# First two chunks' tokens in one load, transposed together ahead of all products

## Chip, cores, metric

One core of a Trainium2 chip runs the whole program. The metric is the device time of one execution in microseconds. Time before: 343.93 us, median of three runs (343.65 to 343.94); the profile of it that is read below is of an execution of 343.26 us. "us from the start" below counts from the start of the profile's span.

## The reference

Two independent attention blocks, A and B, of the same shape, their outputs side by side:

```python
# B=16, Sq=32, D=1024; Hq=32, Hkv=4, Sk=512, Dh=128; all bfloat16
q = (x @ wq).reshape(B, Sq, Hq, Dh).transpose(0, 2, 1, 3)
k, v = (jnp.repeat(c, Hq // Hkv, axis=1) for c in (k_cache, v_cache))
p = softmax(einsum("bhqd,bhkd->bhqk", q, k) * Dh ** -0.5)
o = einsum("bhqk,bhkd->bhqd", p, v).transpose(0, 2, 1, 3).reshape(B, Sq, Hq * Dh)
out = o @ wo          # for A and for B, then concatenate([a, b], axis=-1)
```

## The kernel before

A's tokens x are 512 rows of 1024 values. The product with wq needs x transposed, in eight chunks of 128 columns. The first four chunks come by plain loads (two chunks to a load) and are transposed on PE, the rest by transposing DMAs. While the first loads are on their way, PE runs dummy products on a constant (`warm_up`), because PE starts at a lower clock (the traces below show products 107 ns apart at first and 54 ns later), which activity is to lift. P is 128, TT is 4 (blocks of 128 tokens), DC is 8 chunks, HC is 4, REP is 8 and NF is 6 (heads).

The early loads, all issued by SP in this order:

```python
def load_x(d0, t0, t1):
    nc.sync.dma_start(
        out=x_sb[:, t0:t1, d0 * P:(d0 + 2) * P],
        in_=x_v[:, t0:t1, d0 * P:(d0 + 2) * P],
    )

# ... load_x_transposed and load_w0 cut: a load through the transposing DMA, and a load of weights ...

nc.scalar.preload_act_table_set("natural_log_exp_and_others")
load_x(0, 0, TT // 2)
load_w0(0, 1, 0, NF // 2)
load_x(0, TT // 2, TT)
load_w0(0, 1, NF // 2, NF)
load_w0(1, 2, 0, NF)
load_x(2, 0, TT)
load_w0(2, 3, 0, NF)
load_w0(3, 4, 0, NF)
# ... later loads cut ...
```

PE's order at the start. `first_heads(heads, chunks, t0, t1)` makes the products of these heads and chunks for token blocks t0 to t1, so a full one has 512 columns:

```python
def warm_up(n):
    for _ in range(n):
        nc.tensor.matmul(
            first_q[HALF][:, 0:P], lhsT=warm, rhs=warm, start=True, stop=True
        )

def transpose_x(d, t0, t1, copy, ps=None):
    if ps is None:
        ps = psum.tile([P, NTOK], BF16, name="xT_ps", tag="ob")
    for tt in range(t0, t1):
        nc.tensor.transpose(
            ps[:, tt * P:(tt + 1) * P], x_sb[:, tt, d * P:(d + 1) * P], ident[:]
        )
    ts = slice(t0 * P, t1 * P)
    copy(out=xT[0][:, d, ts], in_=ps[:, ts])

def first_heads(heads, dcs, t0=0, t1=TT):
    ts = slice(t0 * P, t1 * P)
    for dc in dcs:
        for h in heads:
            nc.tensor.matmul(
                first_q[h][:, ts],
                lhsT=w0[dc // HC][:, dc % HC, h * DH:(h + 1) * DH],
                rhs=xT[0][:, dc, ts],
                start=(dc == 0 and t0 == 0),
                stop=(dc == DC - 1),
            )

warm_up(22)
for tt in range(2):
    transpose_x(0, tt, tt + 1, nc.vector.tensor_copy)
transpose_x(1, 0, 2, nc.scalar.copy, spare)
warm_up(2)
first_heads((0, 1, 2), (0,), 0, 1)
transpose_x(0, 2, TT, nc.vector.tensor_copy)
transpose_x(1, 2, TT, nc.scalar.copy)
first_heads((0, 1, 2), (0,), 1, 2)
warm_up(1)
first_heads((0, 1, 2), (0,), 2, TT)
first_heads((3, 4, 5), (0,), 0, 2)
first_heads((3, 4, 5), (0,), 2, TT)
first_heads(range(0, NF - 2), (1,))
transpose_x(2, 0, TT, nc.vector.tensor_copy)
transpose_x(3, 0, TT, nc.scalar.copy)
# ... chunks 2 to 7, then the stream of all other products ...
```

B's tokens come much later, planned into slots of the main loop (about 2.33 us each):

```python
def load_xT_b(d0, d1):
    if d0 == 0:
        xT[1] = blk_tile([P, DC, NTOK], "xT")
    nc.sync.dma_start_transpose(
        out=xT[1][:, d0:d1, :],
        in_=B_x.flatten_outer_dims()[:, d0 * P:d1 * P],
    )

for n in range(2):
    at(GRP * (n + 3) - 2, load_xT_b, n * HC, (n + 1) * HC)
```

## Time and profile before

| what | value | view |
|---|---|---|
| span | 341.5 us | page, first line |
| PE busy | 337.4 us, 99% | page, part 1 |
| chain of waits | PE 99% | page, part 4 |
| PE starts | 0.93 us | timeline |
| first half of the tokens landed | 3.01 us | the trace's issues and landings |
| weights of chunk 1 landed | 6.10 us | the same |
| unbroken stream of products starts | 7.47 us | timeline |
| last product starts | 338.1 us | timeline |

The page of the kernel before: span, busy time of each engine, and the chain of work that ended last.

```profile
span 341.5 us, 5512 instructions
...
PE 337.4 (99%) x2130; PEld 214.4 (63%) x2130; DVE 265.6 (78%) x337; ACT 185.8 (54%) x209; POOL 46.7 (14%) x206
...
PE 99%; ACT 0%; issue 0%; ACTq 0%
```

PE is busy 99% of the time, and everything that ended last is PE's. In the trace, from 7.47 us to the last product, each 512-column product starts 216 ns after the one before it, with no gap. So nothing after 7.47 us can be won by better loads. Only the start can change.

The start on PE, from the timeline (start in us, duration of the group in us, instruction, out<-in, form, count):

```profile
0.93 2.52 PE L516 MATMUL q_ps<-const-bfloat16-1.0 128*128 128x128 bf16 x22 [0.93 <-PEq L700]
3.24 0.63 PE L524 MATMUL xT_ps<-ident,x_sb 128*128 128x128 bf16 x4
3.67 0.42 PE L516 MATMUL q_ps<-const-bfloat16-1.0 128*128 128x128 bf16 x2
3.88 0.53 PE L534 MATMUL q_ps<-xT,w_sb 128*128 128x128 bf16 x3
4.20 0.63 PE L524 MATMUL xT_ps<-ident,x_sb 128*128 128x128 bf16 x4
4.63 0.46 PE L534 MATMUL q_ps<-xT,w_sb 128*128 128x128 bf16 x3
4.93 0.22 PE L516 MATMUL q_ps<-const-bfloat16-1.0 128*128 128x128 bf16 x1
5.00 2.19 PE L534 MATMUL q_ps<-xT,w_sb 128*128 128x256 bf16 x13
7.02 0.61 PE L524 MATMUL xT_ps<-ident,x_sb 128*128 128x128 bf16 x8
7.47 1.70 PE L534 MATMUL q_ps<-xT,w_sb 128*128 128x512 bf16 x7
```

Read it with three things in mind.

- L516 are dummies, L524 transposes, L534 the products of q. Useful work starts at 3.24 us, and three more dummies lie in the middle.
- The durations of matmuls overlap (the four transposes from 3.24 us take up to 0.31 us each but start 107 ns apart), so starts say more. 22 dummies start between 0.93 and 3.13 us (four transposes follow at 3.24), one every 107 ns; the eight transposes from 7.02 to 7.42 us start one every 56 ns. In this execution the step from 107 to 54 ns came at 4.88 us, where the trace's record of the granted clock begins. The page's clock row and the windows view show full clock from the first slice on, although starts are 107 ns apart there: only the starts tell of the slow phase.
- A group of one engine can hide a gap. The 13 products from 5.00 us contain one, from 5.98 to 6.15 us, in which PE has nothing to do.

What ended that gap stands in PE's weight loads (who waited for whom; us in total, times, longest):

```profile
PEld L534 <- DMA w_sb<-in_A_wq_dram: 0.3, 1, 0.3
PEld L524 <- DMA x_sb<-in_A_x_dram: 0.3, 1, 0.3
```

The wait for w_sb is the gap: chunk 1's weights landed at 6.10 us. The wait for x_sb is no loss: the weight load of the next transposes waited for tokens that landed at 6.92 us, but PE was still streaming the product before it and the transposes started on time at 7.02 us.

### The profile page before, as it was taken

What the parts mean: (1) busy time and instruction counts of PE and PEld (TensorE: products, weight loads), DVE (VectorE), ACT (ScalarE), POOL (GpSimd) and SP (SyncE); (2) the same over time, 40 slices, a digit from 0 to 9 for tenths busy, and PEclk for the clock granted to TensorE, in tenths of its full rate; (3) what the DMA queues carried; (4) which work ended last, traced back from release to release, by engine and by line L of the source; (5) the groups of instructions that cost most, each with busy time, mean ns of one, the idle gap of its engine ahead of it and who ended that gap; (6) DMA issues with size and microseconds to landing.
All of it is one profiled execution on the core that took longest, in us unless ns stands there. A gap on an engine that the chain in (4) does not pass through costs nothing.

```text
span 341.5 us, 5512 instructions
## 1 busy us (share of the span) xinstructions
PE 337.4 (99%) x2130; PEld 214.4 (63%) x2130; DVE 265.6 (78%) x337; ACT 185.8 (54%) x209; POOL 46.7 (14%) x206
## 2 busy tenths in 40 slices
PE   8999999999999999999999999999999999999996
PEld 7455666666666666666666666666666666666555
DVE  1046988888988898888888988879888888889540
ACT  3058666666667667666645545555555555555110
POOL 0001110011111111110012221222122101111100
PEclk9999999999999999999999999999999999999999
DMA  6999999989996987999999955998649998440001
GB/s 194 300 192 262 295 264 196 238 244 267 277 247 154 232 232 223 192 313 263 316 272 290 280 148 142 334 270 239 117 109 291 354 186 180 98 113 6 18 18 33
DMA packets 128094, 71.70 MB, mean 210 GB/s; under 512 B 75840, under 2 KB 127296, under 8 KB 128064
## 3 DMA queue, kind: packets, MB, share of 16 engines
q1 hardware_dynamic: 127536, 70.21, 84.3%
q0 software_dynamic: 384, 1.05, 0.8%
q8 instruction: 17, 0.28, 0.3%
q14 instruction: 13, 0.11, 0.1%
q10 hardware_dynamic: 144, 0.07, 0.1%
HBM read 50.86 MB, written 2.10 MB: 155 GB/s over the span
## 4 chain that ended last, share of the span: by engine, by line
PE 99%; ACT 0%; issue 0%; ACTq 0%
PE f_ps L320 32%; PE q_ps L301 28%; PE ob L425 16%; PE s_ps L357 16%; PE q_ps L534 4%; PE q_ps L516 1%; PE xT_ps L524 0%; ACT o_sb L329 0%; ACTq L329 0%
## 5 line engine op out<-in xcount | busy, mean ns | idle before, releaser
L365 ACT ACTIVATE p_sb<-s_ps,shift 128x1024 bf16<-128x1024 f32 x128 | 142.6, 1114 | 97.7 <-PE s_ps L357 85.1
L376 DVE TRANSPOSE_TENSOR_REDUCE parts<-p_sb 128x32 f32<-128x1024 bf16 x128 | 158.7, 1240 | 20.9 <-ACT p_sb L365 19.3
L320 PE MATMUL f_ps<-wo_sb,oT 128*128 128x512 bf16 (+1 forms) x544 | 132.3, 366 | 0.0
L301 PE MATMUL q_ps<-xT,wq_sb 128*128 128x512 bf16 x448 | 116.9, 379 | 0.0
L425 PE MATMUL ob<-p_sb,v_sb 128*128 128x256 bf16 x512 | 76.8, 273 | 0.0
L357 PE MATMUL s_ps<-qT,kT 128*128 128x256 bf16 x512 | 76.8, 273 | 0.0
L320 PEld LDWEIGHTS <-oT 128*128 128x128 bf16 x544 | 53.2, 98 | 35.3
L357 PEld LDWEIGHTS <-kT 128*128 128x128 bf16 x512 | 56.9, 113 | 28.3
L301 PEld LDWEIGHTS <-wq_sb 128*128 128x128 bf16 x448 | 43.8, 98 | 32.2
L425 PEld LDWEIGHTS <-v_sb 128*128 128x128 bf16 x512 | 50.1, 98 | 20.0
L447 DVE TENSOR_TENSOR oT<-r,ob 128x512 bf16<-128x512 f32 x64 | 43.9, 686 | 20.0 <-PE ob L425 19.4
L411 DVE STREAM_TRANSPOSE r<-rall 128x512 f32<-128x512 f32 x64 | 44.2, 691 | 1.1
L309 ACT CAST qT<-q_ps 128x512 bf16<-128x512 f32 x56 | 32.6, 583 | 16.6 <-PE q_ps L301 16.6
L394 POOL COPY half<-cs 64x32 f32<-64x32 f32 x32 | 6.5, 204 | 232.1 <-DVE cs L384 232.0
L329 ACT CAST o_sb<-f_ps 128x512 bf16<-128x512 f32 (+1 forms) x17 | 9.5, 558 | 23.6 <-PE f_ps L320 23.6
L534 PE MATMUL q_ps<-xT,w_sb 128*128 128x512 bf16 (+2 forms) x73 | 14.9, 359 | 0.0
L384 DVE TENSOR_REDUCE cs<-parts 128x32 f32<-128x128 f32 x32 | 12.0, 376 | 1.1
L406 DVE RECIPROCAL rall<-sums 128x32 f32<-128x32 f32 x32 | 10.2, 319 | 3.3 <-POOL sums L403 3.3
L534 PEld LDWEIGHTS <-w_sb 128*128 128x128 bf16 x73 | 7.1, 102 | 6.8 <-DMA w_sb<-in_A_wq_dram 0.3
L566 DVE CAST qT<-q_ps 128x512 bf16<-128x512 f32 x4 | 2.5, 683 | 10.2 <-PE q_ps L534 10.2
L331 POOL DMA_DIRECT2D out_dram<-o_sb x8 | 4.6, 574 | 29.3 <-ACT o_sb L329 29.3
L395 POOL TENSOR_TENSOR half<-half,cs 64x32 f32<-64x32 f32 x32 | 7.8, 243 | 2.6
(25 smaller groups left out, 46.1 us busy)
## 6 DMA issues: line engine op xcount, KB each, us to landing
v_sb<-in_A_v_cache_dram SPq DMA_DIRECT2D x16, 512.0 KB, 5.7
wq_sb<-in_B_wq_dram SPq DMA_DIRECT2D x8, 1024.0 KB, 5.7
wo_sb<-in_A_wo_dram SPq DMA_DIRECT2D x8, 1024.0 KB, 7.1
v_sb<-in_B_v_cache_dram SPq DMA_DIRECT2D x16, 512.0 KB, 4.6
wo_sb<-in_B_wo_dram SPq DMA_DIRECT2D x8, 1024.0 KB, 8.1
wq_sb<-in_A_wq_dram SPq DMA_DIRECT2D x5, 1024.0 KB, 5.9
wq_sb<-in_A_wq_dram SPq DMA_DIRECT2D x2, 512.0 KB, 7.3
kT<-in_A_k_cache_dram SPq DMA_TRANSPOSE x64, 4.4
```

Source lines behind the costliest of these rows:

```text
L301: nc.tensor.matmul(ps[:], lhsT=w[:, dc, (h % 4) * DH:(h % 4 + 1) * DH], rhs=xT[pr][:, dc, :], start=(dc == 0), stop=(dc == DC - 1),)
L309: nc.scalar.copy(out=qT[pr, g][:, :, hl, :], in_=ps[:].rearrange("p (b s) -> p b s", s=SQ),)
L320: nc.tensor.matmul(ps[:, 0:width], lhsT=oT[pr, tt][:, h, :], rhs=wo_tiles[pr, nh, h // REP][:, h % REP, off:off + width], start=(h == 0), ...
L357: nc.tensor.matmul(s_ps[:, c, :], lhsT=kT[:, i % GRP, c, :], rhs=qT[pr, g][:, b, :, :].rearrange("p h s -> p (h s)"), start=True, stop=True,)
L365: nc.scalar.activation(out=p_sb[:], in_=s_ps[:], func=ACTF.Exp, bias=shift[:], scale=SCALE)
L376: nc.vector.tensor_reduce(out=parts[k][:, q, :, :].rearrange("p c h -> p (c h)"), in_=st[i]["p"][:].rearrange("p c (h s) -> p (c h) s", s=SQ),
L384: nc.vector.tensor_reduce(out=cs[:], in_=parts.pop(k)[:].rearrange("p q c h -> p q h c"), axis=AX.X, op=ALU.add,)
L406: nc.vector.reciprocal(out=rall[:, k, :], in_=quad.pop(k)[:])
L411: nc.vector.transpose(out=r[:].rearrange("p n s -> p (n s)"), in_=rall[:, k, o * 2 * REP:(o + 1) * 2 * REP] .unsqueeze(2).to_broadcast([P, ...
L425: nc.tensor.matmul(ob[j][:, q, :], lhsT=v_sb[:, i % GRP, c, :], rhs=st[i]["p"][:, c, :], start=(c == 0), stop=(c == KC - 1),)
L447: nc.vector.tensor_tensor(out=out, in0=rcp.pop(j)[:].rearrange("p (q h) s -> p q h s", h=REP), in1=ob.pop(j)[:].rearrange("p q (h s) -> p ...
L534: nc.tensor.matmul(first_q[h][:, ts], lhsT=w0[dc // HC][:, dc % HC, h * DH:(h + 1) * DH], rhs=xT[0][:, dc, ts], start=(dc == 0 and t0 == 0 ...
```

## The change

The two first token loads of 128 KB become one of 256 KB, so each early load behind them moves up one place in SP's queue. All eight transposes of chunks 0 and 1 come ahead of all products, the dummies all go to the front (23 instead of 22 + 2 + 1). B's tokens are transposed by DMA in three pieces instead of two.

```diff
--- before.py
+++ after.py
@@ -461,11 +461,9 @@
             x_v = A_x.flatten_outer_dims().rearrange("(t p) d -> p t d", p=P)
             wq_v = A_wq.rearrange("(c p) n -> p c n", p=P)
 
-            def load_x(d0, t0, t1):
-                nc.sync.dma_start(
-                    out=x_sb[:, t0:t1, d0 * P:(d0 + 2) * P],
-                    in_=x_v[:, t0:t1, d0 * P:(d0 + 2) * P],
-                )
+            def load_x(d0):
+                ds = slice(d0 * P, (d0 + 2) * P)
+                nc.sync.dma_start(out=x_sb[:, :, ds], in_=x_v[:, :, ds])
 
             def load_x_transposed(d0):
                 nc.sync.dma_start_transpose(
@@ -480,12 +478,11 @@
                 )
 
             nc.scalar.preload_act_table_set("natural_log_exp_and_others")
-            load_x(0, 0, TT // 2)
+            load_x(0)
             load_w0(0, 1, 0, NF // 2)
-            load_x(0, TT // 2, TT)
             load_w0(0, 1, NF // 2, NF)
             load_w0(1, 2, 0, NF)
-            load_x(2, 0, TT)
+            load_x(2)
             load_w0(2, 3, 0, NF)
             load_w0(3, 4, 0, NF)
             load_w0(0, HC, NF, REP)
@@ -539,19 +536,13 @@
                             stop=(dc == DC - 1),
                         )
 
-            warm_up(22)
-            for tt in range(2):
-                transpose_x(0, tt, tt + 1, nc.vector.tensor_copy)
-            transpose_x(1, 0, 2, nc.scalar.copy, spare)
-            warm_up(2)
-            first_heads((0, 1, 2), (0,), 0, 1)
-            transpose_x(0, 2, TT, nc.vector.tensor_copy)
-            transpose_x(1, 2, TT, nc.scalar.copy)
-            first_heads((0, 1, 2), (0,), 1, 2)
-            warm_up(1)
-            first_heads((0, 1, 2), (0,), 2, TT)
-            first_heads((3, 4, 5), (0,), 0, 2)
-            first_heads((3, 4, 5), (0,), 2, TT)
+            warm_up(23)
+            transpose_x(0, 0, TT // 2, nc.vector.tensor_copy)
+            transpose_x(0, TT // 2, TT, nc.vector.tensor_copy)
+            transpose_x(1, 0, TT, nc.scalar.copy, spare)
+            for ts in ((0, TT // 2), (TT // 2, TT)):
+                first_heads(range(0, NF // 2), (0,), *ts)
+            first_heads(range(NF // 2, NF), (0,))
             first_heads(range(0, NF - 2), (1,))
             transpose_x(2, 0, TT, nc.vector.tensor_copy)
             transpose_x(3, 0, TT, nc.scalar.copy)
@@ -609,8 +600,8 @@
                     in_=B_x.flatten_outer_dims()[:, d0 * P:d1 * P],
                 )
 
-            for n in range(2):
-                at(GRP * (n + 3) - 2, load_xT_b, n * HC, (n + 1) * HC)
+            for n, (d0, d1) in enumerate(((0, 2), (2, 5), (5, DC))):
+                at(GRP * (n + 3) - 2, load_xT_b, d0, d1)
             for nh in range(NH):
                 for hg in range(HKV):
                     at(NG - 12 + nh * 8 + hg * 2, load_wo, 0, nh, hg)
```

## The prediction

> **What bounds the kernel now.** The page gives PE 99% busy of a 341.5 us span; the chain of waits is 99% PE. Start to start, the trace's matmuls run without a bubble from 7.47 us to the last at 338.1 us (a 512-column product every 216 ns). So only the time until PE reaches this unbroken stream can change. In the timeline before it, PE starts 22 dummy products at 0.93 us; 128-column instructions start every 107 ns until the granted clock rises at 4.88 us, every 54 to 56 ns after. The Trainium skill ("TensorE: Matmul & The Clock Gate", What's actually happening) says about 3.4 us of sustained activity, in a free-running window, lift the clock; here it took 3.95 us.
>
> Losses after the first tokens land (3.0 us): 3 more dummies (about 0.29 us) and 0.17 us of PE idleness (5.98 to 6.15 us) waiting for chunk 1's weights, which land at 6.10 us. The next chunks' tokens land at 6.92 us, 0.1 us before PE wants them.
>
> **What the change does.** Columns of products and number of transposes are the same. Dummies go from 25 to 23, all in front. Two 128 KB token loads (issued 0.74 and 1.75 us, landed 3.01 and 4.04 us) become one of 256 KB. An issue takes SP 0.43 to 0.50 us whatever its size, so every later early load is issued about 0.48 us sooner: chunk 1's weights at 2.2 instead of 2.73 us, the next tokens at 2.7 instead of 3.20 us. Copies of transposed tokens fall from 7 to 6, all hidden. B's tokens come in 3 pieces instead of 2 in slots where PE has no bubble; the last should land around 73 us and is needed around 83 us (estimate from slots of 2.33 us): no effect.
>
> **On the critical path.** The 256 KB land at about 3.6 us (estimate: the first half-load's 2.27 us plus 128 KB at the 215 GB/s seen from 2 to 3 us). Dummies end at 0.93 + 23 x 0.107 = 3.39 us, so PE idles about 0.2 us. Then 8 transposes and 24 column blocks (32 units of 128) lie before chunk 1: about 12 cold until 4.88 us, 20 warm, ending at about 5.98 us, the same point as now, but with chunk 1's weights landed (about 5.7 us) and the next tokens soon after (about 6.5 us). What is won is the 0.17 us bubble: gain 0.1 to 0.3 us, 0.05%, of the order of the runs' spread (343.65 to 343.94).
>
> **Prediction:** 343.75 us, 343.2 to 344.3. Faster by over 2%: 0.002; within 2%: 0.99; slower by over 2%: 0.008.
>
> **What would show it.** First token load lands at 3.4 to 3.8 us; PE idle 0.1 to 0.4 us before the first transpose; chunk 1's weights land at 5.6 to 5.9 us, no PE idleness before their products; the unbroken stream begins near 7.3 us (now 7.47); afterwards nothing but a shift.
>
> **What would make it wrong.** (1) The clock rises later: the idle gap and eight transposes in a row fall in the activity window, and the skill (same page, Part 4) says transposes do not count as PE-busy; a rise one window (3.4 us) later would cost about 1.5 us. (2) The early loads are limited by bandwidth, not issue (DMA share 0.93 to 0.99 from 4 to 7 us), so they land no sooner: gain near zero. (3) The first load lands after 4.0 us. (4) A later load with little to spare now (chunk 2's weights, 7.43 us) becomes the new wait.

## The result and the profile after

Six runs each: 343.80 us (343.12 to 344.13) against 343.53 us (343.27 to 343.94) before. The ratio is 1.0002, 95% interval 0.9989 to 1.0016: the same. (A ratio here is the mean time of one kernel's runs over the mean of the other's of the same rounds, so not quite the ratio of the medians.)

The page and the start on PE after the change (L513 dummies, L521 transposes, L531 products):

```profile
span 341.4 us, 5456 instructions
...
PE 335.2 (98%) x2083; PEld 213.7 (63%) x2122; DVE 265.5 (78%) x336; ACT 185.6 (54%) x208; POOL 46.7 (14%) x206
...
PE 97%; DMA 1%; issue 1%; ACT 0%; ACTq 0%
```

```profile
0.93 2.63 PE L513 MATMUL q_ps<-const-bfloat16-1.0 128*128 128x128 bf16 x23 [0.93 <-PEq L691]
3.74 1.04 PE L521 MATMUL xT_ps<-ident,x_sb 128*128 128x128 bf16 x8 [0.18 <-DMA x_sb<-in_A_x_dram]
4.57 2.56 PE L531 MATMUL q_ps<-xT,w_sb 128*128 128x256 bf16 x13
6.96 0.61 PE L521 MATMUL xT_ps<-ident,x_sb 128*128 128x128 bf16 x8
7.63 1.70 PE L531 MATMUL q_ps<-xT,w_sb 128*128 128x512 bf16 x7
```

Who waited for whom among PE's weight loads, up to 40 us:

```profile
PEld L521 <- DMA x_sb<-in_A_x_dram: 0.4, 1, 0.4
```

The tokens landed at 3.69 us, and PE idled from 3.35 to 3.74 us (the wait for x_sb, 0.4 us at the weight load). The wait for chunk 1's weights is gone: they landed at 5.79 us, and their first product started at 6.10 instead of 6.15 us. (In this trace the first product of the stream has no record; its weight load at 7.36 us stands where before's stands at 7.42 us. 39 matmul records are missing in all, 2083 beside 2122 weight loads; the other 8 by which the count lies below before's 2130 are two dummies and six products fewer.) The last product starts at 338.04 instead of 338.11 us. So in this pair of executions 0.06 us are won at the start, and nothing after it but that shift.

0.06 us is about a sixteenth of the spread of the changed kernel's runs, which is 1.0 us. The profile says where a gain could lie, but not why six runs of one program differ by 1 us. That became the main question.

### The profile page after: what moved, and what is told of

Read it like the earlier page. It is cut to its first block, busy times and chain, and to the rows that moved or that the text cites. A ratio compares the mean times of both kernels' runs of the same rounds, so it can differ in the third digit from the quotient of the medians.

```text
span 341.4 us, 5456 instructions
## 1 busy us (share of the span) xinstructions
PE 335.2 (98%) x2083; PEld 213.7 (63%) x2122; DVE 265.5 (78%) x336; ACT 185.6 (54%) x208; POOL 46.7 (14%) x206
## 4 chain that ended last, share of the span: by engine, by line
PE 97%; DMA 1%; issue 1%; ACT 0%; ACTq 0%
PE f_ps L320 32%; PE q_ps L301 28%; PE ob L425 17%; PE s_ps L357 16%; PE q_ps L531 4%; DMA x_sb<-in_A_x_dram 1%; PE xT_ps L521 0%; ACT o_sb L329 0%; ACTq L329 0%
## 5 line engine op out<-in xcount | busy, mean ns | idle before, releaser
L320 PE MATMUL f_ps<-wo_sb,oT 128*128 128x512 bf16 (+1 forms) x525 | 128.2, 366 | 0.6
L301 PE MATMUL q_ps<-xT,wq_sb 128*128 128x512 bf16 x430 | 113.2, 379 | 0.5
L531 PE MATMUL q_ps<-xT,w_sb 128*128 128x512 bf16 (+1 forms) x65 | 14.1, 374 | 0.1
L531 PEld LDWEIGHTS <-w_sb 128*128 128x128 bf16 x67 | 6.6, 100 | 6.9
```

The source lines that it names most:

```text
L301: nc.tensor.matmul(ps[:], lhsT=w[:, dc, (h % 4) * DH:(h % 4 + 1) * DH], rhs=xT[pr][:, dc, :], start=(dc == 0), stop=(dc == DC - 1),)
L320: nc.tensor.matmul(ps[:, 0:width], lhsT=oT[pr, tt][:, h, :], rhs=wo_tiles[pr, nh, h // REP][:, h % REP, off:off + width], start=(h == 0), ...
L531: nc.tensor.matmul(first_q[h][:, ts], lhsT=w0[dc // HC][:, dc % HC, h * DH:(h + 1) * DH], rhs=xT[0][:, dc, ts], start=(dc == 0 and t0 == 0 ...
```

## The experiments

Twelve kernels ran, in three groups of four; each group shared a chip and its runs of the kernel before (medians 343.38, 343.29 and 343.38 us). The trace of one execution of each gives this table. "Clock" is when starts change from 107 to 54 ns apart, which is where the record of the granted clock begins (the trace of after_again has no such record, and 6.51 us is read from its starts alone); "chunk 1" is the start of the first product of chunk 1; "stream" is the first weight load after the second group of transposes; "tail" is the time from the last product's start to the end of the span; all in us.

| kernel | first transpose | weights 0, second half | weights 1 | clock | chunk 1 | stream | tail | median (range) |
|---|---|---|---|---|---|---|---|---|
| before | 3.24 | 4.78 | 6.10 | 4.88 | 6.15 | 7.42 | 3.36 | 343.53 (343.27–343.94) |
| before_again | 3.24 | 4.86 | 6.09 | 5.58 | 6.30 | 7.56 | 3.37 | 343.47 (343.26–343.66) |
| pieces_only | 3.24 | 4.86 | 6.09 | 4.83 | 6.13 | 7.40 | 3.79 | 344.04 (343.51–345.48) |
| pieces_again | 3.24 | 4.53 | 6.05 | 6.92 | 6.95 | 8.21 | 3.79 | 344.30 (343.79–344.58) |
| late_split | 3.24 | 4.81 | 6.32 | 3.80 | 6.37 | 7.64 | 3.79 | 344.02 (343.66–344.59) |
| four_loads | 3.24 | 5.65 | 6.79 | 5.18 | 6.84 | 8.11 | 3.73 | 344.44 (344.31–344.56) |
| order_only | 3.35 | 4.84 | 6.07 | 4.87 | 6.12 | 7.38 | 3.37 | 343.37 (343.27–343.51) |
| loads_only | 3.73 | 5.32 | 5.95 | 7.40 | 7.42 | 8.68 | 3.43 | 344.12 (343.65–344.68) |
| after | 3.74 | 5.20 | 5.79 | 5.03 | 6.10 | 7.36 | 3.37 | 343.80 (343.12–344.13) |
| after_again | 3.88 | 5.48 | 6.35 | 6.51 | 6.89 | 8.15 | 3.36 | 343.67 (342.89–344.41) |
| start_only | 3.66 | 5.51 | 6.06 | 4.88 | 6.22 | 7.47 | 3.43 | 343.57 (343.29–343.90) |
| gap_filled | 3.88 | 5.07 | 6.06 | 5.71 | 6.52 | 7.77 | 3.37 | 343.57 (343.38–343.70) |
| no_dummies | 3.65 | 5.32 | 5.91 | 7.20 | 7.04 | 8.38 | 3.37 | 344.73 (343.97–345.20) |
| two_queues | 3.36 | 4.30 | 5.80 | 4.55 | 5.85 | 7.12 | 3.35 | 343.26 (343.06–343.48) |

### The whole change again

No edit. 

> The changed kernel again, unedited, to see how single runs spread. My theory (the body is PE-bound and unchanged, the change moves the start of the unbroken stream by under 0.1 us): ratio 0.999 to 1.001 against before, runs again spread over 0.5 to 1.0 us, and the runs' spans follow something other than the change: the long runs (spans near 342.2) have a granted clock of 0.999, the short ones (341.4) 1.000. Rival (the change makes the start itself unstable, for example by letting the clock rise one window later in some runs): a second group of runs 1 us or more longer in this kernel and not in the one before.

Measured: ratio 1.0005 (0.9990 to 1.0020), six runs from 342.89 to 344.41 us, a wider spread than the 0.5 to 1.0 us expected. Together with the six runs above they form two groups, five at 342.89 to 343.25 us and six at 343.99 to 344.41 us, with one between: much what my rival forecast. The profile of after_again fell on an execution of 344.10 us:

```profile
3.88 1.03 PE L521 MATMUL xT_ps<-ident,x_sb 128*128 128x128 bf16 x8 [0.33 <-DMA x_sb<-in_A_x_dram]
4.71 3.21 PE L531 MATMUL q_ps<-xT,w_sb 128*128 128x256 bf16 x13
```

The same 13 products from 4.71 us take 3.21 us, against 2.56 in the first profile, and no load ends a wait between them. The clock rose at 6.51 instead of 5.03 us. The stream starts 0.79 us later and the span is 0.79 us longer. So between these two executions the difference has its source before 8 us, nearly all of it in the rise of the clock; the rest of the span is a shift. The mean granted clock fits what I expected in five of the six runs (0.999 in two long ones, 1.000 in the three short ones); the sixth is this one, and its 1.000 tells nothing, since its trace has no record of the clock.

### The two parts of the start alone

loads_only is before with

```diff
-            load_x(0, 0, TT // 2)
+            load_x(0, 0, TT)
             load_w0(0, 1, 0, NF // 2)
-            load_x(0, TT // 2, TT)
             load_w0(0, 1, NF // 2, NF)
```

> Before, with the loads of the change (one 256 KB first load, the later ones sooner) and PE's old order. Theory: the first tokens land at about 3.7 us, PE idles about 0.45 us after 22 dummies, the three dummies in the middle still cost, so the first products of chunk 1 start at about 6.2 to 6.3 us (before: 6.15) with their weights long there (about 5.8), and the unbroken stream starts at about 7.5 to 7.6 us (before 7.47): 0 to 0.2 us longer. Rival (issue order is all that matters, sooner loads alone give the gain): stream starts before 7.4 us.

order_only is before with the changed `warm_up(23)` block in place of the old one, and the old loads.

> Before, with the PE order of the change (23 dummies, all transposes first, then products) and the old loads. Theory: transposes of the second half of the tokens wait until 4.04 us, chunk 1's weights still land at about 6.1 us, so products of chunk 1 still start at 6.1 to 6.2 us and the stream at 7.4 to 7.5 us: no gain, the bubble at chunk 1's weights is what binds. Rival (removing two dummies from the middle gives the gain by itself): chunk 1's products start before 6.0 us and the stream before 7.3 us.

The start on PE in loads_only, then in order_only, from their timelines:

```profile
3.73 0.61 PE L523 MATMUL xT_ps<-ident,x_sb 128*128 128x128 bf16 x4 [0.28 <-DMA x_sb<-in_A_x_dram]
...
5.52 2.93 PE L533 MATMUL q_ps<-xT,w_sb 128*128 128x256 bf16 x13
```

```profile
3.35 0.42 PE L524 MATMUL xT_ps<-ident,x_sb 128*128 128x128 bf16 x2
4.08 0.82 PE L524 MATMUL xT_ps<-ident,x_sb 128*128 128x128 bf16 x6 [0.32 <-DMA x_sb<-in_A_x_dram]
4.70 2.45 PE L534 MATMUL q_ps<-xT,w_sb 128*128 128x256 bf16 x13
```

The sooner loads alone: 344.12 us, ratio 1.0018 (1.0005 to 1.0031), stream at 8.68 us. The first transposes started at 3.73 us as expected; the extra microsecond is the clock, which rose at 7.40 us in this execution. The new order alone: 343.37 us, ratio 0.9998 (0.9985 to 1.0011), stream at 7.38 us, as expected: chunk 1's products wait for weights that land at 6.07 us. Neither part shows a gain alone; what the sooner loads would give at an early rise, this one trace cannot say. In the second fence the transposes of the second half wait at 4.08 us, as expected, and the products from 4.70 us take 2.45 us with the wait for chunk 1's weights in them.

### The pieces alone, twice, and an inert edit

pieces_only and pieces_again are before with

```diff
-            for n in range(2):
-                at(GRP * (n + 3) - 2, load_xT_b, n * HC, (n + 1) * HC)
+            for n, (d0, d1) in enumerate(((0, 2), (2, 5), (5, DC))):
+                at(GRP * (n + 3) - 2, load_xT_b, d0, d1)
```

> Before, with B's tokens transposed in three pieces and nothing else. Theory: no bubble on PE near 50 to 90 us, last piece landed over 5 us before its first use, ratio 1.000 within 0.0015. Rival (the third piece delays key loads and gives back what the start wins): 0.1 to 0.3 us longer, with PE idle between 50 and 90 us.

> The three-pieces run again: in its profile the lost time stood at 18.9 and 27.5 us, where A's later weights landed 3 us later than before, and the first changed instruction is issued at 53 us. My theory: it can't be the pieces, so this load lies at 0.999 to 1.001, with PE bubbles, if any, at late weights before 30 us. Rival (the pieces cost 0.5 us, by whatever way): ratio 1.001 to 1.003 again.

late_split is before with one late weight load in two halves, nothing else:

```diff
-                nc.sync.dma_start(
-                    out=t[:],
-                    in_=v[:, hg * REP:(hg + 1) * REP, nh * NW:(nh + 1) * NW],
-                )
+                cuts = (0, HALF, REP) if (pr, nh, hg) == (1, 1, 3) else (0, REP)
+                for a, b in zip(cuts, cuts[1:]):
+                    nc.sync.dma_start(
+                        out=t[:, a:b, :],
+                        in_=v[:, hg * REP + a:hg * REP + b, nh * NW:(nh + 1) * NW],
+                    )
```

> An inert edit: before, with the last weight load of B's output product (issued at about 262 us, needed far later) split in two, so one more DMA and nothing else, no instruction changed before 260 us. If the level of the three-pieces kernel (0.5 to 0.8 us above) belongs to the program as it is loaded or launched and not to the pieces, such an edit can move the level too: median above 343.7 with the clock rising late in the profile. If the level comes of the pieces' work, this one lies at the level of before: 343.3 to 343.6, ratio 1.000 within 0.0008.

Measured: 344.04, 344.30 and 344.02 us; ratios 1.0016 (1.0003 to 1.0029), 1.0021 (1.0007 to 1.0035) and 1.0017 (1.0003 to 1.0031). My expectation of "no cost" for the pieces fell twice, and the inert edit costs as much. So it is not the work of the pieces. (late_split's profile does not have the late clock that I expected of it: it rose at 3.80 us, the earliest of all, and PE then idled 0.70 us for chunk 1's weights.) The last step of the chain of waits (start, duration, what), under the header with the span, shows one part of it, in before and then in pieces_again:

```profile
core 0 of [0], span 341.5 us
...
338.46 0.37 ACT o_sb L329
```

```profile
core 0 of [0], span 342.7 us
...
339.25 0.37 ACT o_sb L329
```

From the end of the last copy to the end of the span it is 341.5 - 338.83 = 2.67 us before and 342.7 - 339.62 = 3.08 us in pieces_again. The last store landed equally long after the last product in both (2.38 and 2.39 us in the trace). After it, SP's sequencer runs through its waits for the DMA semaphores at the end of the program: one wait is left before (at 340.51 us), eight are left in pieces_again (341.30 to 341.73 us), each 60 ns after the last. The program uses eight such semaphores in turn, and the final waits have a fixed order; where the last store's semaphore stands first in that order, seven waits come after it. The tail column bears this out in all fourteen traces: the kernels with one DMA more than before have 3.79 us, with two more 3.73, with one fewer 3.43, with the same number 3.35 to 3.37. So one more DMA, in both places where one was added (B's tokens, B's late weights), costs 0.42 us at the end of this program, and not through any work it does. The whole change removes one load and adds one piece, which leaves the number alone.

The rest of what the three lie above before, 0.2 to 0.6 us of medians, I can't assign from one trace each. In pieces_again it is the clock, which rose at 6.92 us although nothing before 53 us is edited and PE never idled. In pieces_only's slowest execution, which its profile shows, it is late weights:

PE's timeline near 27 us in that execution:

```profile
27.25 0.59 PE L301 MATMUL q_ps<-xT,wq_sb 128*128 128x512 bf16 x2
29.15 1.25 PE L301 MATMUL q_ps<-xT,wq_sb 128*128 128x512 bf16 x5 [1.30 <-DMA wq_sb<-in_A_wq_dram]
```

PE stands still for nearly 1.5 us for A's weights, which landed at 29.1 us (26.1 us in before's trace), long before the edit. The B tokens themselves landed at 75.3 us, 8 us before the first product of B, with no gap on PE there.

### The kernel before against itself

No edit.

> The kernel before under another name, against itself. It says what a ratio means here. If separate loads of one kernel differ in nothing, ratio 1.000 within 0.0005, and then the 1.0016 of the three-pieces run is a real cost. If a load of a program has its own level (for example its buffers' places in memory, so its DMA rate), a ratio of 0.999 to 1.0015 can come from nothing.

343.47 against 343.29 us, ratio 1.0001 (0.9987 to 1.0014). The two are the same within noise, so ratios of 1.0016 and more stand out, if barely. In its trace the clock rose at 5.58 us, and no early load ended a wait on PE.

### The change without the pieces

```diff
-            for n, (d0, d1) in enumerate(((0, 2), (2, 5), (5, DC))):
-                at(GRP * (n + 3) - 2, load_xT_b, d0, d1)
+            for n in range(2):
+                at(GRP * (n + 3) - 2, load_xT_b, n * HC, (n + 1) * HC)
```

> The change without the three pieces: B's tokens in two loads as before. Theory (the start wins about 0.1 us at the same rise of the clock; each execution's own rise of the clock, between 4.5 and 7.4 us, moves the start of the stream by half as much; the pieces cost nothing): runs between 342.9 and 344.4 as in the whole change, ratio 0.999 to 1.001. Rival (the two loads of the three-pieces kernel were slower by 0.16 and 0.21% because of the pieces, which give back what the start wins): ratio 0.998 to 0.9990, no run over 343.6.

343.57 us, ratio 1.0000 (0.9987 to 1.0013), and two runs over 343.6 us: within this noise the pieces neither give back a gain nor hide one. With one DMA fewer the tail is 3.43 us, so the third piece saves 0.06 us. In its trace the clock rose at 4.88 us, as in the first trace of before, and the stream started at 7.47 us against 7.42: this pair of traces with the same rise shows no gain at the start. There is a new wait on the weights (weight loads of PE, who waited for whom; us in total, times, longest):

```profile
PEld L531 <- DMA w_sb<-in_A_wq_dram: 0.6, 2, 0.3
PEld L521 <- DMA x_sb<-in_A_x_dram: 0.4, 1, 0.4
```

One of the two is for the second half of chunk 0's weights. They were issued at 1.79 us, sooner than in before (2.22), and landed later, at 5.51 us (4.78). Ahead of their first product, at 5.56 us, PE idled for 0.22 us; this is in the 13 products' time, 2.75 us against 2.56 in the change's first trace although the clock rose sooner:

```profile
3.66 1.03 PE L521 MATMUL xT_ps<-ident,x_sb 128*128 128x128 bf16 x8
4.49 2.75 PE L531 MATMUL q_ps<-xT,w_sb 128*128 128x256 bf16 x13
```

So point (4) of what could make the prediction wrong came true in this execution, with other weights than I had named.

### Filling the idle time with dummies

The changed kernel with

```diff
-            warm_up(23)
+            warm_up(28)
```

> The changed kernel with 28 instead of 23 dummies, so that PE runs without idleness from 0.93 us until after the first tokens have landed (3.7 to 3.85 us). Theory (the idleness of 0.4 to 0.55 us just before the tokens delays the rise of the clock in part of the executions, at 5.03, about 6.4 and 7.4 us in the profiles with it, 4.83 to 4.88 without): clock rises at 4.8 to 5.0 us, stream starts at 7.4 to 7.5 us, median 343.2 to 343.5, runs within 0.5 us of each other, none over 344.0. Rival (the spread of the changed kernel comes from its loads or from the eight transposes in a row): runs spread over 1 us as before, and the clock rises late in some.

343.57 us, ratio 1.0004 (0.9990 to 1.0017), five runs within 0.32 us and none over 343.70. But the clock rose at 5.71 us and the stream started at 7.77 us, both later than I expected, and together with pieces_again (6.92 us without any idleness) and order_only (4.87 us with 0.5 us of it) this takes the theory down in the form that I gave it, that idleness before the tokens is what makes a rise late. (A finer form, under "The rise of the clock" below, fits all the traces.) The narrow spread of these five runs speaks for an effect of idleness all the same; five runs do not settle it.

### Hardly any dummies

```diff
-            warm_up(23)
+            warm_up(1)
```

> The changed kernel with 1 dummy instead of 23. Theory (the clock rises only after sustained activity of PE): with activity only from 3.7 us on, the clock rises 1.5 to 4 us later than with dummies (between 7 and 9.5 us), every us of that costs half a us at the start of the stream: stream at 8.4 to 9.8 us, 1.0 to 2.3 us longer, 344.5 to 346. Rival (the rise has nothing to do with the dummies, as three different rises under one and the same start of the kernel could be read): rise and time as in the change, 343.0 to 344.4.

The start on PE:

```profile
0.93 0.28 PE L513 MATMUL q_ps<-const-bfloat16-1.0 128*128 128x128 bf16 x1 [0.93 <-PEq L691]
3.65 1.03 PE L521 MATMUL xT_ps<-ident,x_sb 128*128 128x128 bf16 x8 [2.45 <-DMA x_sb<-in_A_x_dram]
4.48 3.67 PE L531 MATMUL q_ps<-xT,w_sb 128*128 128x256 bf16 x13
```

344.73 us, ratio 1.0034 (1.0019 to 1.0048); the clock rose at 7.20 us. The 13 products take 3.67 us instead of 2.56. One rise at 7.20 us would prove little, since loads_only rose at 7.40 us with 22 dummies; that all six runs lie at 343.97 us or above (median 344.73 us; the change's are 343.80 and 343.67) shows that activity matters. Time and rise lie in the range expected, the stream (8.38 us) just below it.

### The reverse of the change, doubled

four_loads is before with the first tokens in four loads:

```diff
-            load_x(0, 0, TT // 2)
+            load_x(0, 0, 1)
+            load_x(0, 1, 2)
             load_w0(0, 1, 0, NF // 2)
-            load_x(0, TT // 2, TT)
+            load_x(0, 2, 3)
+            load_x(0, 3, TT)
             load_w0(0, 1, NF // 2, NF)
```

> The reverse of the change, doubled: before, with the first tokens in four loads of 64 KB, so every later early load is issued one or two places (0.5 to 1.0 us) later. Theory (early loads are limited by issue): chunk 1's weights land at 6.7 to 7.1 us and the next tokens at 7.5 to 7.9 us (6.10 and 6.92 before), PE idle 0.6 us or more before each, the stream starts at 8.1 to 8.5 us: 0.6 to 1.0 us longer. Rival (bandwidth limits, issue order is worth little): both land within 0.3 us of before, stream before 7.8 us, at most 0.3 us longer.

The start on PE:

```profile
5.27 1.26 PE L536 MATMUL q_ps<-xT,w_sb 128*128 128x256 bf16 x9
6.84 1.04 PE L536 MATMUL q_ps<-xT,w_sb 128*128 128x512 bf16 x4 [0.31 <-DMA w_sb<-in_A_wq_dram]
7.71 0.61 PE L526 MATMUL xT_ps<-ident,x_sb 128*128 128x128 bf16 x8
```

344.44 us, ratio 1.0025 (1.0012 to 1.0038). Chunk 1's weights, issued 0.82 us later (3.54 us), landed 0.69 us later (6.79 us); the next tokens landed 0.71 us later (7.63 us). PE idled 0.48 us before chunk 1; ahead of the next tokens it did not idle at all, so they cost less than expected. Of the 1.06 us between the medians the two more DMAs account for 0.37 us in the tail, so the late loads cost about 0.7 us, which agrees with the stream: 8.11 against 7.42 us.

### The two halves from two queues

two_queues is before with the second half of the tokens issued by ACT at the same time:

```diff
+            load_x(0, TT // 2, TT, nc.scalar)
             nc.scalar.preload_act_table_set("natural_log_exp_and_others")
             load_x(0, 0, TT // 2)
             load_w0(0, 1, 0, NF // 2)
-            load_x(0, TT // 2, TT)
             load_w0(0, 1, NF // 2, NF)
```

where `load_x` takes the issuing engine as a fourth argument (cut), and with 22 dummies, then the transposes of the first half, of the second half, then the products as in the change.

> The kernel before with the two halves of the first tokens issued at once, one from SP, one from ACT's queue ahead of its table load, the other early loads one place sooner as in the change, 22 dummies, then transposes of the first half, of the second half, and products. Theory: the halves land at 3.0 to 3.5 us, nearly no idleness ahead of the transposes, clock rises at 4.8 to 5.0 us, chunk 1's products start at 5.75 to 5.95 us with their weights just landed, stream starts at 7.1 to 7.25 us (before 7.47): 0.2 to 0.35 us shorter, runs within 0.5 us. Rival (issue from a second queue slows the loads: bandwidth is what limits): chunk 1's weights land after 6.0 us and the stream starts at 7.35 us or later.

The start on PE:

```profile
3.36 1.15 PE L524 MATMUL xT_ps<-ident,x_sb 128*128 128x128 bf16 x8
4.30 2.58 PE L534 MATMUL q_ps<-xT,w_sb 128*128 128x256 bf16 x13
6.72 0.61 PE L524 MATMUL xT_ps<-ident,x_sb 128*128 128x128 bf16 x8
```

343.26 us (343.06 to 343.48), ratio 0.9997 (0.9983 to 1.0011). Its stream started at 7.12 us, as expected, with a clock that rose early (4.55 us). But the halves landed at 3.31 and 3.73 us: together they took as long as the one load of 256 KB (3.69 us). The Trainium skill ("DMA: Bandwidth & Descriptors", Issuing engines are not separate DMA queues) says that DMAs from several engines run on the same 16 DMA engines and that another queue saves only the issue time; this trace agrees. This is the version that I would keep of those tried, but no run shows it faster beyond noise: the 0.2 to 0.35 us that I expected did not show, and its one trace had an earlier rise of the clock than any expected.

## Why the prediction was right

The time lay in the range, 343.80 against 343.75 us predicted. That the two are so close is luck. The prediction counted its gain of 0.1 to 0.3 us down from 343.93 us, the median of the first three runs of before; with three more runs that median is 343.53 us, so what was measured is no gain that the noise lets us see. And the range, 343.2 to 344.3 us, holds all six runs of before as well. What held is "within noise of before" and most of the reasons for it. Point by point:

**Only the start can change.** Right. In the traces of the change, of order_only and of loads_only there is no gap on PE after the stream has begun. Two other traces have gaps at late weights of A, near 19 and 27 us in pieces_only (1.8 us together) and at 27 us in before_again (0.06 us); no edit reaches there.

**The sum at the start.** Right in its form. Count PE's work between the first transpose and chunk 1 in units of 128 columns: 35 before (three are dummies), 32 after. A unit takes 107 ns before the rise of the clock and 54 ns after it. With first transpose T and rise R, PE reaches chunk 1 at T + 0.495 (R - T) + 0.054 x units, unless a load holds it or chunk 1 comes before the rise. (0.495 is 1 - 54/107; times are taken to the ns.) For after that is 3.74 + 0.64 + 1.73 = 6.11 us (measured 6.10), for after_again 6.91 (6.89), gap_filled 6.51 (6.52), before_again 6.29 (6.30), pieces_again 6.95 (6.95). So at the same rise the change costs 0.505 x (3.74 - 3.24) = 0.25 us by its later start and saves 3 x 0.054 = 0.16 us of dummies: 0.09 us worse where nothing waits for loads. With an early rise before's PE waits for chunk 1's weights until 6.15 us and the change's does not: at before's own rise of 4.88 us the sum gives 6.03 us for the change, so 0.12 us won (an estimate), and more at an earlier rise. The one trace of the change's start with that rise, start_only, doesn't show it: its first product of chunk 1 came at 6.22 us, because the second half of chunk 0's weights held PE for 0.22 us. The later start eats what the dummies give, as predicted. (The prediction's 215 GB/s is not what the windows view gives from 2 to 3 us, 230 GB/s; its estimate of the landing, 3.6 us, stays the same. Measured were 3.69 us, and 0.39 us of idleness instead of 0.2.)

**Sooner issue lands sooner.** The size was off. I had chunk 1's weights at about 5.7 us and the tokens at 6.5 us. In the six traces with the change's loads the weights landed at 5.79 to 6.35 us, mean 6.02, and the next tokens at 6.59 to 7.15 us, mean 6.81. In the six with before's loads the means are 6.12 and 6.91 us. So 0.48 us of sooner issue bought 0.1 us of sooner landing, while 0.82 us of later issue in four_loads cost 0.69 us. So before seems to have sat close to the point where the DMAs and not SP limit the start. Point (2) of what could make the prediction wrong was thus mostly true, and the second half of chunk 0's weights even landed later (5.07 to 5.51 instead of 4.53 to 4.86 us). Why the DMAs move less there is open.

**The rise of the clock.** The term that I had wrong. I took it as fixed at 4.88 us, with a late rise as a chance for the change alone. It came between 3.80 and 7.40 us in fourteen traces, also at a start that is the same as before's (3.80, 4.83, 5.58, 6.92). By the slope above each us of delay moves everything after it by 0.495 us where no load holds PE, so the 3.6 us between the extremes are worth up to 1.8 us: six times the most that the prediction gave the change, 0.3 us. The Trainium skill ("TensorE: Matmul & The Clock Gate", What's actually happening) gives a window that runs freely, which fits a rise that falls differently in each execution; it gives 500 ns either way, and the 3.6 us between our extremes is one whole window of its 3.4 us instead.

The traces tell more about it than I had read from them. Thirteen of them have a record of the granted clock. Full clock lasts 337.92 us in ten of these and 334.51 us in three (pieces_again, loads_only, no_dummies); the two differ by 3.41 us and are 99 and 98 times that. So rise and fall lie on a grid of 3.41 us, and where the grid lies differs between executions of one kernel. Now take from the starts of PE's instructions how much of a step of the grid PE was streaming (107 ns for 128 columns before the rise). In the step before the rise it was 84% or more in all fourteen traces (least in late_split, which rose at 3.80 us); in the step before that, after which the clock did not rise, it was 76% or less (most in pieces_again: its step ended at 3.51 us, too soon after PE's first product at 0.93 us, so it had to wait for 6.92 us). In loads_only a step ended at 3.99 us with 75%; with its 0.49 us of idleness filled it would have been 90% (an estimate from the same starts), but the clock rose a step later, at 7.40 us. So read, chance decides where the grid lies, and idleness before the tokens costs a whole step where a step ends shortly after it, and nothing elsewhere. The transposes count as activity in this: without them the step before the rise in the change's first trace has 64%, which would have lifted the clock, while 68% in pieces_again would not. This fits all fourteen traces (after_again's grid is assumed, since it has no record), but it was read from them afterwards and no run was made to test it.

Before is shielded against a late rise by its wait for weights: by the sum, a rise up to about 5.2 us costs it nothing, so its runs crowd near 343.3 us. In the two traces of the change PE is held by no load once its tokens are there, so a rise pays or costs everywhere. The runs agree: of 12 runs of the change three are under 343.2 us and six over 343.9 us; of 37 runs of before none and four. (The five runs of start_only, with the same start but for the 0.22 us told above, have none of either; these are small numbers.)

What is open: whether the change also makes late rises more frequent. Six of 12 against four of 37 suggest it, though before's wait hides all rises up to 5.2 us; no_dummies shows that much idleness can do it, and gap_filled's narrow runs point the same way. By the grid, the change's 0.4 us of idleness would cost a step in about 0.4 of every 3.41 us, one execution in eight (an estimate, if the grid lies anywhere with equal chance); late rises without idleness, as in pieces_again, come on top. No run tests this share.

**B's pieces have no effect.** Right for PE, wrong in that they have one: by their number. They keep the count of DMAs and so the tail, worth 0.06 us against leaving them out (tail 3.37 against 3.43 us).

## What to carry to other kernels

Where one engine streams without a gap, ask first how much time lies before the stream, and whether what sets it is issue, transfer, or the engine's own clock: here PE at its clock (5.98 us) and the weights (6.10 us) reached chunk 1 within 0.2 us of each other, and moving one only showed the other. For changes worth a tenth of a percent, compare traces at the same rise of the clock and count the DMAs: the rise moved the start of the stream by 0.8 us between two traces of one kernel (7.36 and 8.15 us), and one more DMA moved the end by 0.42 us. An inert edit as a control tells you this before you explain a cost that isn't there.

## What the Trainium skill lacked or had wrong

- "TensorE: Matmul & The Clock Gate", What's actually happening: it gives a transition that varies by 500 ns either way. In the five traces that have before's start, with PE active from 0.93 us on, the rise came at 3.80 to 6.92 us; over all fourteen at 3.80 to 7.40 us. Nor does it say how much of a window must be active: here 76% did not lift the clock and 84% did.
- The same page, Part 4, says that the full clock doesn't engage for transposes. Before's eight transposes at 7.02 to 7.42 us started 56 ns apart, the first four, at 3.24 to 3.56 us, 107 ns apart: they run at whatever clock has been granted. That transposes don't count as activity is not borne out either: see the 64% and 68% above.
- "DMA: Bandwidth & Descriptors", Issuing engines are not separate DMA queues, calls the time to initiate a DMA usually small beside the DMA. That holds for one load here (0.43 to 0.50 us on SP, 2.3 us and more until it has landed), but the section lacks that the times of one queue add up: two more loads ahead cost 0.69 us at the landing of chunk 1's weights.
- No page that I read tells what the waits for DMA semaphores at the end of a program cost: 60 ns each, in a fixed order, so the tail is 3.35 to 3.79 us depending on the number of DMAs.
